# Local attention with a mixture of experts behind it: a tail of at most 32 tokens with the output's columns, in place of the sum, dealt to the four column groups

## The chip, the core and the metric

The kernel runs on one core of one Trainium2 chip. The time is the device time of one execution in microseconds; the number given for a kernel is the median of its runs.

## What is computed

Queries, keys and values have shape 4 x 8 x 768 x 64 (batch, heads, positions, head size). Each position attends to its neighbours closer than 16 positions and to 24 summaries of blocks of 32 positions. The result, read as 3072 tokens of 512 numbers, goes into a layer of eight experts, of which each token takes the two best:

```python
x = attn_out.transpose(0, 2, 1, 3).reshape(3072, 512)
noisy = x @ w_gate + log1p(exp(x @ w_noise)) * noise
top2 = the two largest of noisy per token; top2_w = softmax over those two
for e in range(8):
    for k in range(2):
        mask = top2[:, k] == e
        h = maximum(x[mask] @ w1[e], 0)            # 512 -> 1024
        out[mask] += top2_w[mask, k, None] * (h @ w2[e])   # 1024 -> 512
```

## The kernel before

TensorE (PE) does the attention in 24 tiles of 128 tokens. From about 137 us on the experts are computed, one after the other, the fullest first. Expert e has room for `CAPS[e]` tokens: 800, 832, 808, 800, 784, 776, 768, 768. Its tokens are cut into chunks of 128, and what is over the first 768 is its **tail**, the seventh chunk (`LAST` = 6): 32, 64, 40, 32, 16 and 8 tokens for experts 0 to 5, none for 6 and 7.

For each expert PE makes the hidden values (lines L854 for experts 0 and 1, L1360 for the later ones, which form them by the seven products of Strassen's scheme), ScalarE (ACT) rounds them to f16 in `hth`, and VectorE (DVE) writes the remainder to `htl` (L863, L1395). The second matrix product then goes chunk by chunk into a PSUM bank `pt` (L909, L1432), in three passes of eight matmuls (w2h by hth, w2l by hth, w2h by htl). After a chunk DVE scales it by the gate's weight and adds what other experts have left in the output (`y`, L931; L929 where nothing is added), and GpSimd (POOL) scatters the rows of `y` to the output by an indirect DMA (L90). The rows that are added were gathered by POOL beforehand (`prev`).

A tail does not fill the 128 columns of PE's array, so it is put on parts of the array. With 33 to 64 tokens (experts 1 and 2, lines L906 and L1429) there are two column groups of 64, and each computes half of the output's columns: 48 matmuls of 256 columns. With at most 32 tokens (experts 0, 3, 4 and 5, lines L902 and L1426; the function `four` says which) there are four column groups of 32, and each computes all 512 columns of a quarter of the sum over the hidden values: 24 matmuls of 512 columns. The four partial sums then stand in four groups of 32 partitions, and four operations of DVE add them one after the other:

```python
for g in range(4):
    x = py[32 * g:32 * g + n]
    if g or pv is not None:
        nc.vector.scalar_tensor_tensor(y, x, gw, y if g else pv[:n], op0=OP.mult, op1=OP.add)
```

These are lines L920 and L922. Which rows of the output a 64-wide tail is gathered from and scattered to stands in the table `IL`, and its gate weights in `TL`; `last_ids` (L777, L778) fills both from the table `TB` while PE makes the second half of expert 0's hidden values.

The order of the work is written out by hand, and each engine takes its instructions in that order. Of the loop over f = 0 to 7 for expert 0's second half, each step issues 12 matmuls of PE into one of four banks `h` taken in turn, then ACT's L860, then DVE's L863, which frees the bank. After the step f = 1 DVE also gets the decoding of the token tables (L638 to L694) and `last_ids`; after the steps 2 to 5 a conversion of expert 1's weights (L758). For the experts from 2 on, the first products of the next expert are put ahead of the tail (`seven_head`), and the others follow it; they pass through banks that DVE has to read (L1386, L1388, L1395) before PE can go on writing in them.

Of the kernel before, what the change touches and what calls it, by code (L numbers as in the profile page):

```python
# [8 lines left out]
F32 = mybir.dt.float32  # L9
# [5 lines left out]
OP = mybir.AluOpType  # L15
# [5 lines left out]
P = 128  # L21
TS = S // P
NT = B * TS
N = B * S
DM = H * D
E, F = 8, 1024
# [11 lines left out]
CAPS = (800, 832, 808, 800, 784, 776, 768, 768)  # L38
# [25 lines left out]
def attn_moe(ctx, tc, qt, kt, vt, wgn, noise, w1, w2, out):  # L64
    nc = tc.nc
    PSUM = bass.MemoryType.PSUM

    const = ctx.enter_context(tc.tile_pool(name="const", bufs=1))
# [19 lines left out]
    def indirect(**kw):  # L88
        nc.gpsimd.memset(spacer, 0.0)
        return nc.gpsimd.indirect_dma_start(**kw)  # L90


    LAST = NCH - 1
# [120 lines left out]
    late = []  # L214
# [83 lines left out]
    def bank():  # L298
        return banks[0].tile([P, 1, 512], F32, name="h")
# [206 lines left out]
    TB = const.tile([P, E, NCH, 2], I32, name="tb")  # L506
# [251 lines left out]
        nc.vector.scalar_tensor_tensor(lo, SG[e, i], sc, hi, op0=OP.mult, op1=OP.subtract)  # L758

    XTE = {}  # L760
    HD = DM // 2
    out2 = out.rearrange("n (h d) -> (n h) d", h=2)
    TL = const.tile([P, E, 2], I32, name="tl")
    IL = const.tile([P, E], I32, name="il")
    side = const.tile([P, 1], F32, name="side")

    def last_init():
        nc.gpsimd.memset(TL, OOB)
        nc.gpsimd.memset(side[0:64], 0.0)
        nc.gpsimd.memset(side[64:128], 1.0)  # L770

    def last_ids():
        for c in sorted(set(CAPS)):
            e0, e1 = CAPS.index(c), len(CAPS) - CAPS[::-1].index(c)
            for i in range(2 if c > LAST * P + 32 else 0):
                n = c - LAST * P
                nc.vector.tensor_copy(TL[64 * i:64 * i + n, e0:e1], TB[0:n, e0:e1, LAST, :])  # L777
        nc.vector.tensor_scalar(IL, TL[:, :, 0], 2.0, side, op0=OP.mult, op1=OP.add)  # L778

    def four(e, c):  # L780
        return c == LAST and CAPS[e] - LAST * P <= 32

    def tb_of(e, c):
        return TB0[:, c] if e == 0 and c < 3 else TB[:, e, c]
# [88 lines left out]
    def prev_gather(e, c):  # L873
        n = min(P, CAPS[e] - c * P)
        pv = PREV[pi_[0] % len(PREV)]
        pi_[0] += 1
        if c == LAST and not four(e, c):
            g = indirect(
                out=pv[:, :HD], out_offset=None, in_=out2,
                in_offset=bass.IndirectOffsetOnAxis(ap=IL[:, e:e + 1], axis=0),  # L880
                bounds_check=2 * N - 1, oob_is_err=False)
        else:
            g = indirect(
                out=pv[:n], out_offset=None, in_=out,
                in_offset=bass.IndirectOffsetOnAxis(ap=tb_of(e, c)[:n, 0:1], axis=0),
                bounds_check=N - 1, oob_is_err=False)
        for o in ow.get(e, []):
            tc.declare_no_dep(g.ins, o.ins, reason="an expert's slots hold different tokens")
        ow.setdefault(e, []).append(g)
        return pv  # L890

    def mm2_pass(e, c, py, k, end=2):
        last = c == LAST
        w = WT[e]
        hh, hl = HT
        wn, hx = (("w2h", hh), ("w2h", hl), ("w2l", hh))[k]
        wv = w[wn].rearrange("p a (b d) -> p (a b) d", d=DM)
        for f in range(FC):
            st, sp = k + f == 0, k == end and f == FC - 1
            if four(e, c):  # L900
                g = 32 * (f % 4)
                nc.tensor.matmul(py[g:g + 32], hx[:, f, c * P:c * P + 32], wv[:, f, :], start=k == 0 and f < 4,  # L902
                                 stop=sp, skip_group_check=True)
            elif last:
                for i in range(2):
                    nc.tensor.matmul(py[64 * i:64 * i + 64, :HD], hx[:, f, c * P:c * P + 64],  # L906
                                     wv[:, f, HD * i:HD * i + HD], start=st, stop=sp, skip_group_check=True)
            else:
                nc.tensor.matmul(py, hx[:, f, c * P:c * P + P], wv[:, f, :], start=st, stop=sp)  # L909

    def mm2_out(e, c, py, pv):
        last = c == LAST
        if four(e, c):
            n = CAPS[e] - LAST * P
            y = late[0].tile([P, DM], F32, name="y", bufs=4)[:n]
            gw = tb_of(e, c).bitcast(F32)[:n, 1:2]
            for g in range(4):
                x = py[32 * g:32 * g + n]
                if g or pv is not None:
                    nc.vector.scalar_tensor_tensor(y, x, gw, y if g else pv[:n], op0=OP.mult, op1=OP.add)  # L920
                else:
                    nc.vector.tensor_scalar(y, x, gw, None, op0=OP.mult)  # L922
            y_scatter(e, c, y)
            return
        d = HD if last else DM
        y = late[0].tile([P, DM], F32, name="y", bufs=4)[:, :d]
        gw = (TL[:, e] if last else tb_of(e, c)).bitcast(F32)[:, 1:2]
        if pv is None:
            nc.vector.tensor_scalar(y, py[:, :d], gw, None, op0=OP.mult)  # L929
        else:  # L930
            nc.vector.scalar_tensor_tensor(y, py[:, :d], gw, pv[:, :d], op0=OP.mult, op1=OP.add)  # L931
        y_scatter(e, c, y)
# [5 lines left out]
        mm2_out(e, c, py, pv)  # L938

    def y_scatter(e, c, y):  # L940
        last = c == LAST and not four(e, c)
        n = CAPS[e] - LAST * P if four(e, c) else P
        s = indirect(
            out=out2 if last else out,
            out_offset=bass.IndirectOffsetOnAxis(ap=IL[:, e:e + 1] if last else tb_of(e, c)[:n, 0:1], axis=0),
            in_=y, in_offset=None, bounds_check=(2 * N if last else N) - 1, oob_is_err=False)
        for o in ow.get(e, []):
            tc.declare_no_dep(s.ins, o.ins, reason="an expert's slots hold different tokens")
        ow.setdefault(e, []).append(s)
# [189 lines left out]
    for i in range(3):  # L1139
        x = late[0].tile([P, DM], F32, name=f"prev{i}")  # L1140
# [80 lines left out]
    py = [bank()[:, 0] for c in range(3)]  # L1221
# [34 lines left out]
    def tail(e):  # L1256
        return (CAPS[e] - LAST * P) // 2 if CAPS[e] > LAST * P else 0
# [147 lines left out]
    def cols(e, c, hx, f):  # L1405
        h, k = CAPS[e] // 2, tail(e)
        if c == LAST:
            return hx[:, f, 3 * P:3 * P + (32 if four(e, c) else 64)]
        c0 = P * c if c < 3 else h + k + P * (c - 3)
        return hx[:, f, c0:c0 + P]  # L1410

# [5 lines left out]
    def mm2_part(e, c, py, k, fs, start, stop):  # L1417
        w = G["w2"] if e > 1 else WT[e]
        wn, hx = (("w2h", HT[0]), ("w2h", HT[1]), ("w2l", HT[0]))[k]
        wv = w[wn].rearrange("p a (b d) -> p (a b) d", d=DM)  # L1420
        for f in fs:
            st, sp = start and f == fs[0], stop and f == fs[-1]
            x = cols(e, c, hx, f)
            if four(e, c):
                g = 32 * (f % 4)
                nc.tensor.matmul(py[g:g + 32], x, wv[:, f, :], start=start and f < 4, stop=sp, skip_group_check=True)  # L1426
            elif c == LAST:
                for i in range(2):
                    nc.tensor.matmul(py[64 * i:64 * i + 64, :HD], x, wv[:, f, HD * i:HD * i + HD], start=st,  # L1429
                                     stop=sp, skip_group_check=True)  # L1430
            else:
                nc.tensor.matmul(py, x, wv[:, f, :], start=st, stop=sp, skip_group_check=True)  # L1432

# [55 lines left out]
    for e in range(1, E):  # L1489
        pv = []  # L1490
# [5 lines left out]
        n = e + 1  # L1496
# [45 lines left out]
        else:  # L1542
# [7 lines left out]
            for i in range(1, 5):  # L1550
# [16 lines left out]
                else:  # L1567
                    py = psum.tile([P, 512], F32, name="pt", bufs=2)
# [11 lines left out]
        for c in range(chunks(e)):  # L1580
            if c == chunks(e) - 1 and n < E:
                seven_head(n)
            if c or e == 1:
                py = psum.tile([P, 512], F32, name="pt", bufs=2)
                for i, k in enumerate((0, 2, 1)):
                    if e == 1:
                        mm2_pass(e, c, py, k, 1)
                    else:
                        mm2_part(e, c, py, k, range(FC), i == 0, i == 2)
                    if i < 2:  # L1590
                        hook(32 + 3 * c + i)
            else:
                for k in (2, 1):
                    mm2_part(e, 0, py, k, range(7), False, False)
                    hook(33 - k // 2)
                for k in (0, 2, 1):
                    mm2_part(e, 0, py, k, (7,), False, k == 1)
            mm2_out(e, c, py, pv[c])
            prev()
            hook(34 + 3 * c)  # L1600
# [106 lines left out]
```

## Time and profile before

| | before |
|---|---|
| median of 3 runs | 648.92 us (647.35 to 651.18) |
| profiled execution | 650.73 us, of which the span 648.9 us |
| PE busy | 628.6 us (97% of the span) |
| DVE busy | 481.2 us (74%) |
| ACT busy | 316.1 us (49%) |
| POOL busy | 250.2 us (39%) |

A row of a group of matmuls gives the time from its first start to its last modelled end, and matmuls overlap; so the pace of matmuls is read from the distance of their starts. "Idle before" in square brackets is idle time of that engine just ahead of the row, with what ended it. PEld are loads of stationary weights into PE's array; they run beside matmuls.

### The profile page before, as it was taken

What the parts mean: (1) busy time and instruction counts of PE and PEld (TensorE: products, weight loads), DVE (VectorE), ACT (ScalarE), POOL (GpSimd) and SP (SyncE); (2) the same over time, 40 slices, a digit from 0 to 9 for tenths busy, and PEclk for the clock granted to TensorE, in tenths of its full rate; (3) what the DMA queues carried; (4) which work ended last, traced back from release to release, by engine and by line L of the source; (5) the groups of instructions that cost most, each with busy time, mean ns of one, the idle gap of its engine ahead of it and who ended that gap; (6) DMA issues with size and microseconds to landing.
All of it is one profiled execution on the core that took longest, in us unless ns stands there. A gap on an engine that the chain in (4) does not pass through costs nothing.

```text
span 648.9 us, 14149 instructions
## 1 busy us (share of the span) xinstructions
PE 628.6 (97%) x5295; PEld 363.4 (56%) x5295; DVE 481.2 (74%) x1039; ACT 316.1 (49%) x692; POOL 250.2 (39%) x432
## 2 busy tenths in 40 slices
PE   8989898999999999999999999999999999999995
PEld 7778676765554554465446544554454455445542
DVE  5768598979887599368887887988798679767510
ACT  4878597973054354065436433653465256425300
POOL 4352043202335353623572356326632542333041
PEclk9999798999999999999999999999999999999998
DMA  9999978963639595838786688769776868763021
GB/s 304 325 278 342 307 218 275 299 230 124 198 123 252 166 220 144 282 84 170 185 226 172 168 200 246 181 135 225 236 201 136 221 210 165 175 191 123 3 94 51
DMA packets 123709, 127.93 MB, mean 197 GB/s; under 512 B 83242, under 2 KB 86674, under 8 KB 123630
## 3 DMA queue, kind: packets, MB, share of 16 engines
q1 hardware_dynamic: 111838, 90.66, 52.1%
q0 software_dynamic: 11792, 36.27, 18.2%
q8 instruction: 44, 0.72, 0.5%
q14 instruction: 35, 0.29, 0.2%
HBM read 81.85 MB, written 25.61 MB: 166 GB/s over the span
## 4 chain that ended last, share of the span: by engine, by line
PE 86%; DVE 6%; ACT 3%; DMA 2%; issue 2%; SPq 1%; POOL 0%; POOLq 0%; DVEq 0%; ACTq 0%
PE pt L1432 29%; PE h L1360 16%; PE h L854 10%; PE pt L909 7%; PE pt L1360 3%; PE pt L341 3%; PE o L1360 3%; PE s L318 3%; PE o L354 3%; PE h L909 2%; PE o L246 1%; ACT p L333 1%; PE pt L378 1%; DMA vd<-in_vt_dram 1%; DVE y L920 1%
## 5 line engine op out<-in xcount | busy, mean ns | idle before, releaser
L90 POOL DMA_INDIRECT out_dram<-y,tb x52 | 69.5, 1336 | 165.3 <-DVE y L931 127.7
L90 POOL DMA_INDIRECT xg<-xd,tb x54 | 60.9, 1127 | 118.8 <-DVE rh L1388 31.5
L1432 PEld LDWEIGHTS <-hth 128*128 128x128 f16 x576 | 56.3, 98 | 66.7
L931 DVE SCALAR_TENSOR_TENSOR y<-pt,tb,prev 128x512 f32<-128x512 f32 x42 | 31.5, 749 | 64.9 <-PE pt L1432 54.2
L1360 PEld LDWEIGHTS <-w1h 128*128 128x128 f16 x504 | 48.9, 98 | 38.2 <-issue 4.4
L1432 PE MATMUL pt<-w2l,hth 128*128 128x512 f16 x288 | 69.0, 379 | 0.0
L1432 PE MATMUL pt<-w2h,htl 128*128 128x512 f16 x288 | 69.0, 379 | 0.0
L1432 PE MATMUL pt<-w2h,hth 128*128 128x512 f16 x288 | 69.0, 379 | 0.0
L1360 PEld LDWEIGHTS <-w1l 128*128 128x128 f16 x504 | 49.3, 98 | 34.9
L90 POOL DMA_INDIRECT prev<-out_dram,tb x45 | 52.6, 1169 | 23.9 <-issue 13.2
L333 ACT ACTIVATE p<-s,nm 128x120 f32<-128x120 f32 x192 | 51.1, 377 | 0.8
L854 PE MATMUL h<-xte,w1h 128*128 128x384 f16 (+2 forms) x248 | 49.1, 336 | 0.0
L1432 PEld LDWEIGHTS <-htl 128*128 128x128 f16 x288 | 28.2, 98 | 34.0
L1349 ACT ACTIVATE w1h<-stg 128x768 f16<-128x768 f32 (+1 forms) x24 | 22.7, 944 | 40.6 <-DVE stg L1340 40.6
L1392 ACT ACTIVATE hth<-h 128x384 f16<-128x384 f32 (+4 forms) x48 | 23.8, 497 | 35.5 <-PE h L1360 35.5
L1349 ACT ACTIVATE w1l<-stg 128x768 f16<-128x768 f32 (+1 forms) x24 | 22.5, 942 | 37.3 <-DVE stg L1340 37.3
L1360 PE MATMUL h<-xte,w1h 128*128 128x384 f16 (+4 forms) x180 | 39.7, 329 | 0.7 <-DVE h L1386 0.4
L1360 PE MATMUL h<-xte,w1l 128*128 128x384 f16 (+4 forms) x180 | 39.7, 329 | 0.0
L1313 ACT ACTIVATE x<-xt 128x512 f16<-128x512 f32 (+2 forms) x44 | 26.5, 626 | 23.4 <-issue 19.2
L1340 DVE TENSOR_TENSOR stg<-stg 128x256 f32<-128x256 f32 x96 | 36.3, 419 | 0.8
L344 ACT ACTIVATE pts<-pt 120x512 f32<-120x512 f32 x48 | 26.7, 609 | 19.4 <-PE pt L341 19.4
L854 PEld LDWEIGHTS <-w1h 128*128 128x128 f16 x256 | 24.7, 98 | 19.5 <-issue 1.2
(301 smaller groups left out, 1305.7 us busy)
## 6 DMA issues: line engine op xcount, KB each, us to landing
stg<-in_w_dram SPq DMA_DIRECT2D x64, 512.0 KB
q<-in_qt_dram SPq DMA_DIRECT2D x24, 256.0 KB
xd<-x SPq DMA_DIRECT2D x24, 256.0 KB
out_dram<-xg SPq DMA_DIRECT2D x8, 768.0 KB
kb<-in_kt_dram SPq DMA_DIRECT2D x6, 768.0 KB
hth<-in_vt_dram SPq DMA_DIRECT2D x12, 260.0 KB
htl<-in_vt_dram SPq DMA_DIRECT2D x16, 195.0 KB
ve<-in_vt_dram SPq DMA_DIRECT2D x12, 260.0 KB
```

Source lines behind the costliest of these rows:

```text
L90: return nc.gpsimd.indirect_dma_start(**kw)
L333: nc.scalar.activation(PE_[t][:, a, hp, :], SC[t][:, a, hp, :], AF.Exp, bias=NM[t][:, 1, a, hp:hp + 1], scale=0.125)
L344: nc.scalar.activation(PT[t][:NK, a], pt[:NK], AF.Copy)
L854: nc.tensor.matmul(ph[:, :n], w1_of(w, wn, c, f), x[:, xo + c, c0:c1], start=(k == 0), stop=(k == 11))
L909: nc.tensor.matmul(py, hx[:, f, c * P:c * P + P], wv[:, f, :], start=st, stop=sp)
L931: nc.vector.scalar_tensor_tensor(y, py[:, :d], gw, pv[:, :d], op0=OP.mult, op1=OP.add)
L1313: nc.scalar.activation(t[:r, c:c + k], src, AF.Copy)
L1340: nc.vector.tensor_tensor(o, x, y, op=op)
L1349: nc.scalar.activation(hi, x, AF.Copy, scale=W1S)
L1360: nc.tensor.matmul(ph[:, :h], w[:, la, a, P * j:P * j + P], x[:, j, :h], start=start and k == 0, stop=k == 5, skip_group_check=True)
L1392: nc.scalar.activation(hh[:, f, t], src, AF.Relu)
L1432: nc.tensor.matmul(py, x, wv[:, f, :], start=st, stop=sp, skip_group_check=True)
```

## The change

Tails of at most 32 tokens now work as the 64-wide ones do: each of the four column groups computes a quarter of the output's columns (128) over the whole sum. A tail thus has 96 matmuls of 128 columns, each with a weight load of its own, in place of 24 of 512; DVE evacuates it with one operation on 128 partitions x 128 columns; and rows of 512 bytes, a quarter of an output row, are gathered and scattered by ids in `IL`. `last_ids` fills the tables expert by expert, with four copies for each of the experts 0, 3, 4 and 5, two for 1 and 2, and one operation for the ids of each. The table `side`, set by POOL, has two columns in place of one.

```diff
     def last_ids():
-        for c in sorted(set(CAPS)):
-            e0, e1 = CAPS.index(c), len(CAPS) - CAPS[::-1].index(c)
-            for i in range(2 if c > LAST * P + 32 else 0):
-                n = c - LAST * P
-                nc.vector.tensor_copy(TL[64 * i:64 * i + n, e0:e1], TB[0:n, e0:e1, LAST, :])
-        nc.vector.tensor_scalar(IL, TL[:, :, 0], 2.0, side, op0=OP.mult, op1=OP.add)
+        for e in range(E):
+            n = CAPS[e] - LAST * P
+            if n > 0:
+                q = parts(e)
+                for i in range(0, P, P // q):
+                    nc.vector.tensor_copy(TL[i:i + n, e], TB[0:n, e, LAST, :])
+                nc.vector.tensor_scalar(IL[:, e:e + 1], TL[:, e, 0:1], float(q), side[:, q // 4:q // 4 + 1],
+                                        op0=OP.mult, op1=OP.add)
+
+    def parts(e):
+        return 4 if CAPS[e] - LAST * P <= 32 else 2
...
-            if four(e, c):
-                g = 32 * (f % 4)
-                nc.tensor.matmul(py[g:g + 32], x, wv[:, f, :], start=start and f < 4, stop=sp, skip_group_check=True)
-            elif c == LAST:
-                for i in range(2):
-                    nc.tensor.matmul(py[64 * i:64 * i + 64, :HD], x, wv[:, f, HD * i:HD * i + HD], start=st,
-                                     stop=sp, skip_group_check=True)
+            if c == LAST:
+                q = parts(e)
+                n, d = P // q, DM // q
+                for i in range(q):
+                    nc.tensor.matmul(py[n * i:n * i + n, :d], x, wv[:, f, d * i:d * i + d], start=st, stop=sp,
+                                     skip_group_check=True)
...
-        if four(e, c):
-            n = CAPS[e] - LAST * P
-            y = late[0].tile([P, DM], F32, name="y", bufs=4)[:n]
-            gw = tb_of(e, c).bitcast(F32)[:n, 1:2]
-            for g in range(4):
-                x = py[32 * g:32 * g + n]
-                if g or pv is not None:
-                    nc.vector.scalar_tensor_tensor(y, x, gw, y if g else pv[:n], op0=OP.mult, op1=OP.add)
-                else:
-                    nc.vector.tensor_scalar(y, x, gw, None, op0=OP.mult)
-            y_scatter(e, c, y)
-            return
-        d = HD if last else DM
+        d = DM // parts(e) if last else DM
```

How the order of DVE's instructions moves at the two places of which the prediction speaks:

DVE in expert 0's second half, from the last step of the token tables (L694) to the first remainder behind `last_ids` (`htl`, L863 before and L865 now). Before:

```order
L694 CAST tb<-ids 128x49
L777 COPY tl<-tb 40x2 x2
L777 COPY tl<-tb 64x2 x2
L778 TENSOR_SCALAR il<-tl,side 128x8
L863 SCALAR_TENSOR_TENSOR htl<-h,hth 128x416
```

The same place now:

```order
L694 CAST tb<-ids 128x49
L778 COPY tl<-tb 32x2 x4
L779 TENSOR_SCALAR il<-tl,side 128x1
L778 COPY tl<-tb 64x2 x2
...
L778 COPY tl<-tb 8x2 x4
L779 TENSOR_SCALAR il<-tl,side 128x1
L865 SCALAR_TENSOR_TENSOR htl<-h,hth 128x416
```

Each of the six experts with a tail has a group of copies (L778) with one L779 behind it. The remainder of step f = 2 has 26 operations ahead of it that fill the tables, in place of 5.

DVE around the tail of expert 3 (`y` is the evacuation, `o`, `h` and `pt` are PSUM banks of expert 4's products, L1353 and L1340 convert weights). Before:

```order
L1353 SCALAR_TENSOR_TENSOR w1l_2961<-stg,w1l_2961 128x1024
L920 SCALAR_TENSOR_TENSOR y<-pt,tb,prev_2970 32x512
L920 SCALAR_TENSOR_TENSOR y<-pt,tb,y 32x512 x3
L1395 SCALAR_TENSOR_TENSOR htl<-o,hth 128x392
L1386 TENSOR_TENSOR h<-h,p_5853 128x392
L758 SCALAR_TENSOR_TENSOR w2l_322<-stg,w2h_321 128x1024 x2
L1388 TENSOR_TENSOR rh_3827<-h,p_5853 128x392
```

Now:

```order
L1340 SCALAR_TENSOR_TENSOR w1l_2967<-stg,w1l_2967 128x1024
L919 SCALAR_TENSOR_TENSOR y<-pt,tl,prev_2976 128x128
L1382 SCALAR_TENSOR_TENSOR htl<-o,hth 128x392
L1373 TENSOR_TENSOR h<-h,p_5949 128x392
L758 SCALAR_TENSOR_TENSOR w2l_322<-stg,w2h_321 128x1024 x2
L1375 TENSOR_TENSOR rh_3923<-h,p_5949 128x392
```

Three operations are gone from between the tail and expert 4's first remainder; the rest stands as it did.

## Rows read from the trace of the kernel before

**Rows 1.** The page's busy time of each engine, with its share of the span and its count of instructions.

```profile
PE 628.6 (97%) x5295; PEld 363.4 (56%) x5295; DVE 481.2 (74%) x1039; ACT 316.1 (49%) x692; POOL 250.2 (39%) x432
```

**Rows 2.** Busy time by stage: the stretch, its length, busy time and count of PE, PEld, DVE, ACT and POOL, PE's clock as a share of full speed, the DMA engines' share, GB/s. The first stretch holds expert 0's second half and its second product, the others reach from tail to tail.

```profile
175.00:210.00 35.00, 35.00 (x210) 17.98 (x208) 28.67 (x57) 15.78 (x23) 15.05 (x23) 1.00 0.71 180
343.00:404.00 61.00, 61.00 (x337) 31.00 (x338) 50.15 (x87) 30.45 (x52) 29.63 (x46) 1.00 0.75 190
404.00:465.00 61.00, 60.70 (x337) 30.91 (x336) 52.18 (x90) 30.28 (x52) 29.79 (x46) 1.00 0.77 194
465.00:526.00 61.00, 60.64 (x341) 31.07 (x339) 48.66 (x84) 28.12 (x48) 25.25 (x42) 1.00 0.76 197
526.00:588.00 62.00, 61.57 (x331) 32.22 (x330) 49.42 (x86) 29.83 (x51) 20.05 (x30) 1.00 0.69 172
```

**Rows 3.** The chain that ended last: start, length on the chain, engine and line. The tails of experts 0, 2 and 3.

```profile
208.50 1.41 PE pt L902 x24
...
340.24 2.74 PE pt L1429 x48
...
402.55 1.44 PE pt L1426 x24
```

**Rows 4.** The timeline of all engines from the tail of expert 3: start, length (us), engine, line, operation, output<-inputs, shape, count, and idle time ahead of it.

```profile
403.89 0.84 PE L1360 MATMUL o<-xte,w1h 128*128 128x392 f16 x4
404.01 0.74 DVE L920 SCALAR_TENSOR_TENSOR y<-pt,tb,prev 32x512 f32<-32x512 f32 x1 [1.53 <-PE pt L1426]
...
404.78 2.31 DVE L920 SCALAR_TENSOR_TENSOR y<-pt,tb,y 32x512 f32<-32x512 f32 x3
...
407.13 0.57 DVE L1395 SCALAR_TENSOR_TENSOR htl<-o,hth 128x392 f16<-128x392 f32 x1
...
407.55 0.49 PE L1360 MATMUL h<-xl,w1l 128*128 128x392 f16 x2
407.61 0.56 DVE L1386 TENSOR_TENSOR h<-h,p 128x392 f32<-128x392 f32 x1
...
408.08 2.35 DVE L758 SCALAR_TENSOR_TENSOR w2l<-stg,w2h 128x1024 f16<-128x1024 f32 x2
408.23 0.82 PE L1360 MATMUL h<-xte,w1h 128*128 128x392 f16 x4 [0.19 <-DVE h L1386]
...
413.86 0.49 PE L1360 MATMUL o<-xl,w1h 128*128 128x392 f16 x2
414.47 0.82 PE L1360 MATMUL h<-xte,w1h 128*128 128x392 f16 x4
```

**Rows 5.** PE's timeline at the same two places behind the tail of expert 5.

```profile
529.36 0.49 PE L1360 MATMUL h<-xl,w1l 128*128 128x384 f16 x2
...
530.10 0.81 PE L1360 MATMUL h<-xte,w1h 128*128 128x384 f16 x4 [0.25 <-DVE h L1386]
...
535.62 0.49 PE L1360 MATMUL o<-xl,w1h 128*128 128x384 f16 x2
536.29 0.81 PE L1360 MATMUL h<-xte,w1h 128*128 128x384 f16 x4 [0.18 <-DVE htl L1395]
```

**Rows 6.** Line L931 of DVE: count, shortest, median and longest duration in ns, starts, shapes.

```profile
L931 DVE SCALAR_TENSOR_TENSOR y<-pt,tb,prev x42: 732/751/753, 251.2 to 641.6; 128x512 f32<-128x512 f32 x42
L931 DVE SCALAR_TENSOR_TENSOR y<-pt,tl,prev x2: 484/484/485, 280.2 to 343.0; 128x256 f32<-128x256 f32 x2
```

**Rows 7.** DVE's timeline around `last_ids` and at the remainder of step f = 7, and L777's line of durations.

```profile
185.66 0.69 DVE L777 COPY tl<-tb 40x2 int32<-40x2 int32 x4
186.46 0.23 DVE L778 TENSOR_SCALAR il<-tl,side 128x8 int32<-128x8 int32 x1
186.60 0.58 DVE L863 SCALAR_TENSOR_TENSOR htl<-h,hth 128x416 f16<-128x416 f32 x1
...
196.43 0.58 DVE L863 SCALAR_TENSOR_TENSOR htl<-h,hth 128x416 f16<-128x416 f32 x1
...
L777 DVE COPY tl<-tb x4: 160/162/164, 185.7 to 186.2; 40x2 int32<-40x2 int32 x2, 64x2 int32<-64x2 int32 x2
```

**Rows 8.** PE's timeline in the same stretch: the last four matmuls of step f = 5 with the first four of f = 6, and the third pass of chunk 3, which reads the remainders.

```profile
187.88 1.57 PE L854 MATMUL h<-xte,w1h 128*128 128x416 f16 x8
...
196.25 1.89 PE L909 MATMUL pt<-w2h,htl 128*128 128x512 f16 x8
```

**Rows 9.** Starts of matmuls on column groups: the tail of expert 3 (first pass, and its weight loads as PEld), and the attention's 64-column matmuls, which go in turn to two column groups.

```profile
402.48 0.61 PE L1426 MATMUL pt<-w2h,hth 128*32 128x512 f16 x8
402.48 0.34 PEld L1426 LDWEIGHTS <-hth 128*32 128x32 f16 x12 [0.32 <-issue]
...
402.92 0.60 PE L1426 MATMUL pt<-w2l,hth 128*32 128x512 f16 x8
...
59.06 0.22 PE L354 MATMUL o<-ve,pts 120*64 120x65 f32 x1
59.07 0.22 PE L354 MATMUL o<-htl,pts 120*64 120x65 f32 x1
59.12 0.22 PE L354 MATMUL o<-ve,pts 120*64 120x65 f32 x1
...
59.88 0.22 PE L354 MATMUL o<-ve,pts 120*64 120x65 f32 x1
```

**Rows 10.** The stretch of the attention in which loads and matmuls stood densest, columns as in rows 2.

```profile
37.32:40.15 2.83, 2.83 (x102) 2.55 (x102) 0.54 (x3) 2.30 (x9) 0.00 (x0) 1.00 1.04 338
```

More of the change, by code (lines that the diff above doesn't have):

```diff
@@ L760, in attn_moe @@
     XTE = {}
-    HD = DM // 2
-    out2 = out.rearrange("n (h d) -> (n h) d", h=2)
+    outs = {q: out.rearrange("n (h d) -> (n h) d", h=q) for q in (2, 4)}
     TL = const.tile([P, E, 2], I32, name="tl")
     IL = const.tile([P, E], I32, name="il")
-    side = const.tile([P, 1], F32, name="side")
+    side = const.tile([P, 2], F32, name="side")
     def last_init():
         nc.gpsimd.memset(TL, OOB)
-        nc.gpsimd.memset(side[0:64], 0.0)
-        nc.gpsimd.memset(side[64:128], 1.0)
+        for i in range(4):
+            for k in range(2):
+                nc.gpsimd.memset(side[32 * i:32 * i + 32, k:k + 1], float(i if k else i // 2))
     def last_ids():
-        for c in sorted(set(CAPS)):
-            e0, e1 = CAPS.index(c), len(CAPS) - CAPS[::-1].index(c)
-            for i in range(2 if c > LAST * P + 32 else 0):
-                n = c - LAST * P
-                nc.vector.tensor_copy(TL[64 * i:64 * i + n, e0:e1], TB[0:n, e0:e1, LAST, :])
-        nc.vector.tensor_scalar(IL, TL[:, :, 0], 2.0, side, op0=OP.mult, op1=OP.add)
-    def four(e, c):
-        return c == LAST and CAPS[e] - LAST * P <= 32
+        for e in range(E):
[8 more added lines that the diff above has]
+        return 4 if CAPS[e] - LAST * P <= 32 else 2
     def tb_of(e, c):
@@ L876, in prev_gather @@
         pi_[0] += 1
-        if c == LAST and not four(e, c):
+        if c == LAST:
             g = indirect(
-                out=pv[:, :HD], out_offset=None, in_=out2,
+                out=pv[:, :DM // parts(e)], out_offset=None, in_=outs[parts(e)],
                 in_offset=bass.IndirectOffsetOnAxis(ap=IL[:, e:e + 1], axis=0),
-                bounds_check=2 * N - 1, oob_is_err=False)
+                bounds_check=parts(e) * N - 1, oob_is_err=False)
         else:
@@ L899, in mm2_pass @@
             st, sp = k + f == 0, k == end and f == FC - 1
-            if four(e, c):
-                g = 32 * (f % 4)
-                nc.tensor.matmul(py[g:g + 32], hx[:, f, c * P:c * P + 32], wv[:, f, :], start=k == 0 and f < 4,
-                                 stop=sp, skip_group_check=True)
-            elif last:
-                for i in range(2):
-                    nc.tensor.matmul(py[64 * i:64 * i + 64, :HD], hx[:, f, c * P:c * P + 64],
-                                     wv[:, f, HD * i:HD * i + HD], start=st, stop=sp, skip_group_check=True)
+            if last:
+                q = parts(e)
+                n, d = P // q, DM // q
+                for i in range(q):
+                    nc.tensor.matmul(py[n * i:n * i + n, :d], hx[:, f, c * P:c * P + n],
+                                     wv[:, f, d * i:d * i + d], start=st, stop=sp, skip_group_check=True)
             else:
@@ L940, in y_scatter @@
     def y_scatter(e, c, y):
-        last = c == LAST and not four(e, c)
-        n = CAPS[e] - LAST * P if four(e, c) else P
+        last = c == LAST
         s = indirect(
-            out=out2 if last else out,
-            out_offset=bass.IndirectOffsetOnAxis(ap=IL[:, e:e + 1] if last else tb_of(e, c)[:n, 0:1], axis=0),
-            in_=y, in_offset=None, bounds_check=(2 * N if last else N) - 1, oob_is_err=False)
+            out=outs[parts(e)] if last else out,
+            out_offset=bass.IndirectOffsetOnAxis(ap=IL[:, e:e + 1] if last else tb_of(e, c)[:, 0:1], axis=0),
+            in_=y, in_offset=None, bounds_check=(parts(e) * N if last else N) - 1, oob_is_err=False)
         for o in ow.get(e, []):
@@ L1407, in cols @@
         if c == LAST:
-            return hx[:, f, 3 * P:3 * P + (32 if four(e, c) else 64)]
+            return hx[:, f, 3 * P:3 * P + P // parts(e)]
         c0 = P * c if c < 3 else h + k + P * (c - 3)
@@ L1423, in mm2_part @@
             x = cols(e, c, hx, f)
-            if four(e, c):
-                g = 32 * (f % 4)
-                nc.tensor.matmul(py[g:g + 32], x, wv[:, f, :], start=start and f < 4, stop=sp, skip_group_check=True)
-            elif c == LAST:
-                for i in range(2):
-                    nc.tensor.matmul(py[64 * i:64 * i + 64, :HD], x, wv[:, f, HD * i:HD * i + HD], start=st,
-                                     stop=sp, skip_group_check=True)
+            if c == LAST:
+                q = parts(e)
+                n, d = P // q, DM // q
+                for i in range(q):
+                    nc.tensor.matmul(py[n * i:n * i + n, :d], x, wv[:, f, d * i:d * i + d], start=st, stop=sp,
+                                     skip_group_check=True)
             else:
```

## The prediction

> **What bounds the kernel now.** I read the page's busy times first: PE is busy for 97% of the span and DVE for 74% [rows 1]. An average does not say which of them a change of a tail touches, so the busy time by stage came next: in expert 0's second half and from expert 2's tail to expert 3's PE has no idle time at all, and in the three stretches behind the tails of experts 3, 4 and 5 it has 0.30, 0.36 and 0.43 us [rows 2]. The clock there is 1.00, the level of 2.4 GHz. So in these stages PE's work is the time: a microsecond more on PE is a microsecond at the end, and a microsecond saved on DVE is worth something only where PE waits for it. The chain of waits shows what a tail costs PE: 1.41 to 1.44 us with four column groups, 2.74 with two [rows 3]. The timelines then show where PE waits for DVE.
>
> **The change, part by part.**
>
> *PE in the tails.* Now four matmuls, one on each column group, start together: eight make a pass, and the passes start at 402.48 and 402.92, so two fours take 0.43 us and one 0.216, which is 512 columns at 2.4 GHz (213 ns) and 2 to 3 ns. Twelve weight loads start within the first 0.34 us less one load's length, ahead of the matmuls that need them [rows 9]. Of the 1.44 us six fours take 1.30; 0.14 is the drain at the end. After the change there are 24 fours of 128 columns. If columns set the pace, a four takes 53 ns and 2.5, and the tail 24 x 0.056 + 0.14 = 1.48 us: 0.04 more than now. If loads and matmuls come at the densest pace that the attention holds over as many of them, 102 pairs in 2.83 us or 27.7 ns a pair [rows 10], the tail takes 96 x 0.0277 + 0.14 = 2.80 us, 1.4 more. Those are the two ends. Between them the nearest row is the attention's 64-column product: two column groups start 7 to 10 ns apart, each with its own load, and the next two follow after 58 to 59 ns (14 steps from 59.06 to 59.88) [rows 9]. Two loads of 64 columns in that time are as many columns of weights as four of 32. I take 58.6 ns for a four: 24 x 0.0586 + 0.14 = 1.55 us, **0.1 us more a tail and 0.4 for four.**
>
> The Trainium skill speaks against the change here: "TensorE: Matmul & The Clock Gate", Part 3, has it that LDWEIGHTS overlaps with matmuls in flight only where the row groups differ, and here all four column groups use all rows; by its formula for LDWEIGHTS a load of 32 columns takes 27 ns, so 96 of them would take 2.6 us, an estimate from that page, and the four tails would cost 5 us more in place of 0.4. The trace speaks against the rule: twelve loads start beside eight matmuls of the same rows [rows 9].
>
> *DVE behind the tails.* The first of four evacuations starts at 404.01 and the last ends at 407.09, 3.08 us in all [rows 4]. One operation of 128 partitions x 128 columns takes their place. The operation takes 751 ns for 512 columns and 484 for 256 [rows 6]; the same slope gives 484 - 134 = 350 ns for 128. So DVE is free 2.7 us earlier. What that is worth is read from PE: behind expert 3's tail the remainder L1395 waits until 407.13 for the chain, L1386 follows at 407.61, and PE, whose next matmul would start at 407.55 + 2 x 0.165 = 407.88, starts at 408.23, after L1386: 0.35 us lost. The two conversions L758 behind it pass the delay on, and at 414.47 PE loses another 0.28 (414.19 was due) [rows 4]. Behind expert 5's tail the same two losses are 0.42 (529.68 due, 530.10 done) and 0.35 (535.94 due, 536.29 done) [rows 5]. For expert 4 I take the mean, 0.70. Together 2.1 us. Behind the two-way tail of expert 2, where one operation of 484 ns evacuates [rows 6], PE has no idle time [rows 2]; so all of it should go: **-2.1 us.** If PE's tail becomes longer, DVE only has more time, and nothing else is late next: L1386 then waits for PE's own product. Expert 0's tail has no such loss to give back [rows 2].
>
> *The tables.* `last_ids` has 26 small operations on DVE where it had 5. The four copies, the wait and the operation for the ids took from 185.66 to 186.60, 0.94 us [rows 7]. After the change four experts need such a group each, and two need one with two copies less (a copy is 0.16 to 0.18 us): 4 x 0.94 + 2 x 0.60 = 4.96, which is 4.0 us more. Copies at their bare 162 ns and ids in 0.14 would give 3.1 more; a third of a microsecond for every operation of ids with its wait, 4.7. Queued behind them is DVE's whole line, without a gap from there to the remainder of step f = 7 [rows 7]. Who waits for it: step f = 6 of PE writes in the bank that the remainder of f = 2 frees. That remainder ends at 186.60 + 0.58 = 187.18, and f = 6 starts at 187.88 + 4 x 0.175 = 188.58 [rows 7, 8]: 1.4 us of cover. The next edge is tighter: the remainder of f = 7 ends at 197.01 [rows 7], and the third pass of chunk 3 wants it in its last matmul, at 196.25 + 7 x 0.216 = 197.76 [rows 8]; with the load ahead of it some 0.6 us of cover. PE thus stands still for 4.0 - 1.4 = 2.6 us at f = 6 and for 0.8 more in chunk 3: **+3.4 us** (2.5 to 4.1 by the two ends), and from there to 404 us no idle time of PE takes it up [rows 2].
>
> *The rest.* Six more small memsets on POOL stand at the end of the attention, where nothing waits for POOL's tables until `last_ids`, 55 us later. Gathers and scatters of a tail now have 128 rows of 512 bytes; they are hidden by the distance between a tail and its next reader, half an expert. I cost both at nothing.
>
> **The sum:** +0.4 - 2.1 + 3.4 = **+1.7 us**, on the profiled execution 650.73 + 1.7 = 652.4. That execution lies 1.8 above the median of the runs shown, so the forecast against the median is 648.92 + 1.7 = **650.6 us**, 0.3% slower, which a measurement of this kernel, that can tell about 0.5% (3.2 us) from no change, would call the same.
>
> **The rivals.**
>
> *Pace of small pairs (0.25).* PE cannot feed a load and a matmul to its column groups every 14 ns, and the tails run at the pace of rows 10: 1.4 us more each, 5.6 for four. Then 5.6 - 2.1 + 3.4 = +6.9, 655.8 us. It decides for slower by 0.5% from a tail of 1.44 + (3.2 + 2.1 - 3.4)/4 = 1.92 us on, a pair each 18.5 ns. For it: no stretch of the attention shows a denser run as long. Against it: those stretches are full with their own columns, so they bound the pace from above only. The skill's rule above is of this kind.
>
> *Stalls stay (0.13).* The losses behind the tails come from the conversions L758 as much as from the evacuation, and PE keeps them: 0.4 + 3.4 = +3.8, 652.7 us. Against it: the stretch behind the two-way tail, with the same conversions, has no idle time [rows 2].
>
> *Tables hidden (0.10).* The small operations overlap so far, or the bank is free so early, that PE does not wait: 0.4 - 2.1 = -1.7, 647.2 us, faster but less than can be told. Against it: DVE's line has no gap in which to make 3 us good.
>
> **How the numbers follow.** The forecast has 0.52 and by its own bounds (2.5 to 4.1 for the tables, 0.04 to 0.3 a tail) reaches from 649.2 to 652.2. The range is to take in the third case, half of the second's way from the forecast to 655.8, and the spread of a median: **647.8 to 655.0**. What is left out is the lower half of "tables hidden" and the full price of the pace. Slower by over 0.5% is nearly all of the pace, most of "stalls stay" and a tail of the forecast: 0.36. Faster by over 0.5% would need tables at no cost and more gain than the losses add up to: 0.04. The same: 0.60.
>
> **What would show it right or wrong.** The four tails on the chain: 1.5 us each by the forecast, 2.8 by the pace. PE's idle time behind the tails of experts 3, 4 and 5: none. In step f = 6 of expert 0's second half: PE idle for 2 to 3 us on DVE's remainder, and again for under 1 us in the third pass of chunk 3. The one evacuation: about 350 ns. The forecast is wrong if a tail is over 1.9 us, if the idle time behind the tails stays, or if PE runs through f = 6.

## The result, and the profile after

| | median us | ratio to before (95%) |
|---|---|---|
| before | 647.14 | |
| changed | 650.79 | 1.0055 (1.0035 to 1.0076) |

The changed kernel is 3.65 us slower, 0.55%, and the interval of the ratio does not take in 1. The forecast was 650.6 and the median lies within its range, but as a difference the forecast was +1.7 us. That the median comes out 0.2 us from the forecast is luck: the median of before, over more executions, is 1.8 us lower than the one the forecast started from. So the difference is what has to be explained. The profiled executions differ by about the same amount: 654.55 us (span 652.8) against 650.73 (span 648.9).

The page of the changed kernel, busy time of each engine, for [rows 1]:

```profile
PE 627.0 (96%) x5583; PEld 364.7 (56%) x5583; DVE 475.7 (73%) x1048; ACT 316.6 (48%) x692; POOL 251.8 (39%) x438
```

PE has 288 matmuls more, 96 for 24 in each of four tails, and is not busy for longer; DVE is busy 5.5 us less. The span is 3.9 us longer all the same, so the time went into waiting.

The busy time by stage, with the columns of [rows 2]:

```profile
175.00:214.00 39.00, 36.08 (x285) 18.93 (x284) 33.13 (x78) 15.86 (x23) 14.70 (x23) 1.00 0.71 158
404.00:465.00 61.00, 60.17 (x405) 31.46 (x403) 48.84 (x87) 29.47 (x52) 29.50 (x47) 1.00 0.80 194
465.00:526.00 61.00, 60.52 (x410) 31.91 (x409) 46.78 (x81) 29.05 (x49) 25.76 (x44) 1.00 0.79 193
526.00:588.00 62.00, 61.91 (x421) 32.95 (x420) 46.21 (x80) 28.96 (x50) 22.20 (x32) 1.00 0.75 183
```

Expert 0's second half now has 2.92 us without a matmul, where it had none. The other three stretches still have idle time, but it has moved, as the timelines below show.

DVE's timeline around `last_ids`, for [rows 7]:

```profile
185.19 0.67 DVE L778 COPY tl<-tb 32x2 int32<-32x2 int32 x4
...
190.12 0.21 DVE L779 TENSOR_SCALAR il<-tl,side 128x1 int32<-128x1 int32 x1
190.25 0.58 DVE L865 SCALAR_TENSOR_TENSOR htl<-h,hth 128x416 f16<-128x416 f32 x1
```

And PE's at step f = 6 and in the third pass of chunk 3, for [rows 8]:

```profile
187.60 0.87 PE L856 MATMUL h<-xte,w1h 128*128 128x416 f16 x4
190.89 0.34 PE L856 MATMUL h<-xte,w1h 128*128 128x416 f16 x1 [2.42 <-DVE htl L865]
...
200.73 0.39 PE L909 MATMUL pt<-w2h,htl 128*128 128x512 f16 x1 [0.50 <-DVE x L815]
```

DVE's remainder of step f = 7, which that last matmul reads:

```profile
200.09 0.58 DVE L865 SCALAR_TENSOR_TENSOR htl<-h,hth 128x416 f16<-128x416 f32 x1
```

`last_ids` now holds DVE from 185.19 to 190.25, 5.06 us. The remainder behind it ends at 190.83, and the next matmul starts at 190.89 after 2.42 us of waiting. In the third pass of chunk 3 the last matmul waits 0.50 us. The row names L815, DVE's operation just ahead of the remainder of f = 7; the remainder itself ends at 200.67, 0.06 us before the matmul starts.

The chain that ended last at the tail of expert 0 and, piece by piece, the tail of expert 3, for [rows 3]:

```profile
211.48 1.45 PE pt L906 x96
...
405.50 0.78 PE pt L1415 x46
...
406.29 0.53 PE pt L1415 x23
406.82 0.35 issue
407.18 0.28 PE pt L1415 x4
407.45 0.46 issue
407.92 0.53 PE pt L1415 x23
```

Expert 0's 96 matmuls take 1.45 us, 0.04 more than its 24 took. Expert 3's take 2.95. "issue" is time in which PE waits for nothing that the profile shows: no semaphore holds it, and the next matmul of the same tail comes late.

PE, POOL and DVE around that tail, for [rows 4, 9]; POOL's lines are its indirect transfers, and their length is the time of the issue:

```profile
404.78 1.53 POOL L90 DMA_INDIRECT xg<-xd,tb  x1 [0.22 <-issue]
...
405.43 0.63 PE L1415 MATMUL pt<-w2h,hth 128*32 128x128 f16 x32
...
405.89 0.87 PE L1415 MATMUL pt<-w2l,hth 128*32 128x128 f16 x32
...
406.62 1.01 POOL L90 DMA_INDIRECT out_dram<-y,tb  x1 [0.22 <-issue]
407.18 0.28 PE L1415 MATMUL pt<-w2h,htl 128*32 128x128 f16 x4 [0.35 <-issue]
...
408.49 0.35 DVE L919 SCALAR_TENSOR_TENSOR y<-pt,tl,prev 128x128 f32<-128x128 f32 x1 [3.05 <-PE pt L1415]
```

The one evacuation takes 0.35 us, as forecast. The gather at 404.78 ends at 406.31, and PE's first halt ends at 406.29; the scatter at 406.62 ends at 407.63, and the last halt ends 0.29 later. The halt between them ends at 407.18, while the scatter is still being issued, and only four pairs run before the next. That coincidence was read out of the trace only after the first experiments; it is what the later ones test.

**The account.** PE's matmuls outside the four-way tails are the same in both kernels, so the start of one and the same matmul can be compared between the two traces:

| the matmul | before | after | lag | change of the lag |
|---|---|---|---|---|
| step f = 1 of expert 0's second half | 177.66 | 177.39 | -0.27 | |
| first of chunk 3 | 192.80 | 195.10 | +2.30 | +2.57, tables |
| tail of expert 0 | 208.43 | 211.41 | +2.98 | +0.68, tables |
| first behind it | 209.84 | 212.87 | +3.03 | +0.05 |
| tail of expert 3 | 402.48 | 405.43 | +2.95 | -0.08 |
| first behind it | 403.89 | 408.38 | +4.49 | +1.54, tail |
| tail of expert 4 | 463.53 | 467.40 | +3.87 | -0.62, losses gone |
| first behind it | 464.94 | 469.66 | +4.72 | +0.85, tail |
| tail of expert 5 | 524.37 | 528.40 | +4.03 | -0.69, losses gone |
| first behind it | 525.78 | 530.19 | +4.41 | +0.38, tail |
| last of the kernel | | | +3.66 | -0.75, losses gone |

Tables +3.25, tails +2.82, losses behind the tails -2.06, the rest -0.08: +3.93 from the first row on. The forecast had +3.4, +0.4 and -2.1. One of its three terms failed.

### The profile page after: what moved, and what is told of

It reads as the page before. It is cut to its first block, busy times and chain, and to the rows that moved or that the text cites. A ratio compares the mean times of both kernels' runs of the same rounds, so it can differ in the third digit from the quotient of the medians.

```text
span 652.8 us, 14739 instructions
## 1 busy us (share of the span) xinstructions
PE 627.0 (96%) x5583; PEld 364.7 (56%) x5583; DVE 475.7 (73%) x1048; ACT 316.6 (48%) x692; POOL 251.8 (39%) x438
## 4 chain that ended last, share of the span: by engine, by line
PE 86%; DVE 7%; DMA 4%; issue 2%; ACT 1%; SPq 0%; POOL 0%; POOLq 0%; DVEq 0%; ACTq 0%
PE pt L1418 29%; PE h L1347 18%; PE h L856 9%; PE pt L909 7%; PE o L1347 4%; PE pt L1347 4%; PE h L909 2%; PE pt L341 2%; PE o L354 2%; PE s L318 2%; DMA htl<-in_vt_dram 2%; PE pt L1415 1%; PE pt L378 1%; DMA stg<-in_w_dram 1%; DVE nm L325 1%
## 5 line engine op out<-in xcount | busy, mean ns | idle before, releaser
L90 POOL DMA_INDIRECT out_dram<-y,tb x48 | 66.6, 1387 | 152.0 <-DVE y L919 131.2
L90 POOL DMA_INDIRECT prev<-out_dram,tb x42 | 48.6, 1156 | 28.0 <-issue 12.8
L1382 DVE SCALAR_TENSOR_TENSOR htl<-h,hth 128x384 f16<-128x384 f32 (+4 forms) x48 | 26.7, 564 | 12.4 <-ACT hth L1379 11.1
```

Source lines behind the costliest of these rows:

```text
L1382: nc.vector.scalar_tensor_tensor(hl[:, f, t], src, 0.0, hh[:, f, t], op0=OP.max, op1=OP.subtract)
```

## The experiments

The median of each kernel, the ratio to before on the same chip, and how much its lag against before grows in the two traces from step f = 1 of expert 0's second half to the last matmul:

| kernel | median us | ratio (95%) | growth of the lag, us |
|---|---|---|---|
| changed | 650.79 | 1.0055 (1.0035 to 1.0076) | +3.93 |
| e1_shift | 650.52 | 1.0047 (1.0021 to 1.0073) | +4.19 |
| e2_spread | 652.60 | 1.0073 (1.0047 to 1.0098) | +8.13 |
| e3_tables_late | 647.46 | 1.0003 (0.9981 to 1.0025) | +1.51 |
| e4_one_evacuation | 644.27 | 0.9960 (0.9932 to 0.9988) | -2.09 |
| e5_pool_after | 647.30 | 1.0010 (0.9985 to 1.0034) | +2.02 |
| e6_pool_copies | 650.05 | 1.0060 (1.0026 to 1.0094) | +2.08 |
| e7_both | 643.67 | 0.9948 (0.9919 to 0.9977) | -2.11 |
| e8_tail0_late | 650.96 | 1.0094 (1.0059 to 1.0129) | +4.01 |

Before was 647.14 beside the changed kernel and e1 to e4, and 646.28 beside e5 to e8. The attention varies by some us between executions: at step f = 1 of expert 0's second half the profiled execution of e1_shift was 6.85 us ahead of that of before, with the same work but the warm-up. So terms of a few tenths are read from the lag between matmuls, not from the medians.

**e1_shift: is it a place in PE's stream?**

```
-    warm_up(WARM)
+    warm_up(WARM - 24)
+    for i in range(86):
+        nc.tensor.matmul(VO[0][:, i % 2, 0:8], identb, identb[:, 0:8], ...
```

> The changed kernel with 62 more pairs of load and matmul on PE: 24 of the 100 warm-up pairs become 86 pairs of 8 columns, so everything behind them stands 124 instructions later in PE's stream, and the work is the same. Theory A (PE takes its instructions in blocks of 256, the 16 kB packets of queue q8, and halts where a block ends; in a tail of 192 short instructions the halt shows): the halts move by 62 pairs. They stood after 73, 32 and 45 pairs of the tails of experts 3, 4 and 5 and 2 matmuls behind that of expert 0; they would stand after 11 pairs of expert 3's tail (hidden by the instructions queued ahead), before those of experts 4 and 5 or at their ends, and after some 35 pairs of expert 0's. Tails of 1.5 us for experts 3 to 5 in place of 2.95, 2.25 and 1.79, and 2.0 to 2.3 for expert 0 in place of 1.45. The whole: 1.5 to 2.5 us less than the changed kernel, if the attention's halts don't move against it. Theory B (the instructions ahead are used up and new ones come at a fixed pace): nothing moves; 2.9, 2.3, 1.8 us again and 1.45 for expert 0.

Measured, PE and POOL around the tail of expert 3:

```profile
397.98 1.53 POOL L90 DMA_INDIRECT xg<-xd,tb  x1 [0.22 <-issue]
...
398.62 0.63 PE L1417 MATMUL pt<-w2h,hth 128*32 128x128 f16 x32
...
399.81 1.01 POOL L90 DMA_INDIRECT out_dram<-y,tb  x1 [0.22 <-issue]
400.39 0.28 PE L1417 MATMUL pt<-w2h,htl 128*32 128x128 f16 x4 [0.38 <-issue]
...
401.16 0.55 PE L1417 MATMUL pt<-w2h,htl 128*32 128x128 f16 x25 [0.50 <-issue]
```

The halts stand after 46, 67 and 71 pairs; they had stood after 46, 69 and 73, and should have moved by 62. In the tail of expert 4 they stand after 24 and 29 pairs in place of 32, in that of expert 5 after 35 in place of 45. Theory A has fallen. Expert 0's tail has none again, 1.45 us.

**e2_spread: long matmuls between the passes.**

```
-            if c == chunks(e) - 1 and n < E:
+            apart = e > 1 and c == LAST and parts(e) == 4
+            if c == chunks(e) - 1 and n < E and not apart:
                 seven_head(n)
...
                     if i < 2:
                         hook(32 + 3 * c + i)
+                        if apart:
+                            seven(n, 0, (1, 5)[i])
```

> The changed kernel, but the two products of the next expert (6 matmuls of 384 to 392 columns each, about 1 us each) that stand ahead of the tails of experts 3, 4 and 5 stand between the tail's three passes. Both theories of the halts inside the tails have it that PE's queue is full again after 1 us of long matmuls; a pass is 32 pairs, 0.45 us. Each pass is then 0.45 to 0.5 us, the 2.8 us of halts in the three tails go to under 0.6, and the time is 2 to 2.8 us under the changed kernel (about 648.3 where that is 650.8). If the halts come from something else (DVE or ACT at the same memory, the bank that the tail writes), they stay: no difference.

Measured: both theories had expected it faster, and it is not. The median is 1.8 us above that of the changed kernel, which the two intervals don't tell apart. In the traces the three tails cost 6.2 us of lag, where those of the changed kernel cost 2.8. POOL at expert 3's tail:

```profile
401.22 1.22 POOL L90 DMA_INDIRECT xg<-xd,tb  x1 [0.22 <-issue]
...
402.82 1.73 POOL L90 DMA_INDIRECT out_dram<-y,tb  x1 [0.29 <-issue]
```

And PE there:

```profile
401.35 0.68 PE L1415 MATMUL pt<-w2h,hth 128*32 128x128 f16 x32
403.24 0.33 PE L1347 MATMUL o<-xte,w1h 128*128 128x392 f16 x1 [1.22 <-issue]
403.96 0.66 PE L1347 MATMUL o<-xte,w1h 128*128 128x392 f16 x3 [0.40 <-issue]
...
404.88 0.63 PE L1415 MATMUL pt<-w2l,hth 128*32 128x128 f16 x32
```

After one pass of 32 pairs PE halts in front of long matmuls, for 1.22 and 0.40 us, and goes on at its full pace afterwards. These long matmuls write another bank (`o`, not `pt`), and the profile shows no semaphore that they wait for, so what is late seems to be not a matmul's data or bank but the instruction itself, whatever its size. A reading that fits: the first pass, now 2 us earlier, has used up what PE held while POOL issues a gather and a scatter. Theory B, a fixed pace, does not fit either: behind the halts 32 pairs run in 0.45 us. Laying the halts of all kernels beside POOL's timeline gave theory D, as e5_pool_after puts it.

**e3_tables_late: the tables alone.**

```
-    def last_ids():
-        for e in range(E):
+    def last_ids(es):
+        for e in es:
...
-            last_ids()
+            last_ids((0,))
...
             on(0, tail_ids)
+            on(1, last_ids, (1, 2))
+            on(2, last_ids, (3, 4))
+            on(3, last_ids, (5,))
```

> The changed kernel, but only expert 0's group of last_ids (4 copies and one operation, 0.8 us) stays where it was; the other 21 small operations stand in the first half of expert 1, where DVE has idle time. My theory: step f = 6 and the third pass of chunk 3 have no idle time any more, so 3.2 us less than the changed kernel, 647.5 where that is 650.8. Rival (DVE's line is late anyway, and PE finds the next thing late): under 1.5 us less.

Measured: 3.3 us less than the changed kernel (647.46 and 650.79, both beside 647.14), and both waits are gone. Expert 0's second half, columns as in [rows 2]:

```profile
175.00:207.00 32.00, 32.00 (x261) 16.90 (x259) 25.81 (x52) 15.34 (x22) 14.44 (x21) 1.00 0.75 184
```

PE has no idle time there, and none in the 34 us behind it, into which the 21 operations have gone: where DVE has time they cost nothing. In the lag the whole is only 2.4 us less. The tables' 3.25 are gone, but the tails cost 1.0 more: expert 4's now meets a gather and a scatter of POOL as expert 3's does, halts after 46, 70 and 74 pairs and takes 3.00 us.

**e4_one_evacuation: the losses behind the tails alone.**

```
-            for g in range(4):
+            for g in range(1):
                 x = py[32 * g:32 * g + n]
```

> The kernel before with the first of the four evacuations of each four-way tail alone; the other three quarters of those tails' sums are left out. The matmuls and the tables are those of before. My theory: PE's losses behind the tails of experts 3, 4 and 5 (0.63, 0.69 and 0.75 us) go, 2.1 us less than before, 645.1 where that is 647.1. Rival (the conversions behind the tail cause them as much): under 1 us less, and the idle times stay in part.

Measured: 0.9960, 2.6 us less than before (0.8 to 4.4); in the lag between matmuls it is 2.1, at the very places of [rows 4, 5]. The stretches behind the tails of experts 3 and 5:

```profile
399.00:460.00 61.00, 61.00 (x349) 31.13 (x342) 49.90 (x87) 30.80 (x54) 28.54 (x47) 1.00 0.80 198
...
520.00:582.00 62.00, 62.00 (x338) 32.67 (x335) 48.02 (x83) 30.76 (x53) 20.09 (x30) 1.00 0.71 174
```

No idle time is left, nor in the one between. The conversions L758 are still there, so "stalls stay" falls.

**e5_pool_after: POOL's transfers away from the tails.**

```
-        y_scatter(e, c, y)
+        if e > 1 and c == LAST - 1 and CAPS[e] > LAST * P and parts(e) == 4:
+            held.append((e, c, y))
+        else:
+            y_scatter(e, c, y)
+            while held:
+                y_scatter(*held.pop())
...
-            on(42 if e == 1 else 47, xs_gather, n + 1, 1)
+            on(42 if e == 1 else 52 if CAPS[e] > LAST * P and parts(e) == 4 else 47, xs_gather, n + 1, 1)
```

> The changed kernel, with POOL's indirect transfers kept away from the tails of experts 3, 4 and 5: the scatter of chunk 5 stands behind the tail's scatter in POOL's line, and the two gathers of the expert after next behind both. PE's and DVE's lines are as they were. Theory D (while POOL issues an indirect transfer, PE gets hardly any new instructions and lives on those it holds, some 64, which a tail uses up in 0.45 us; in the traces so far the halts inside the tails end within 0.3 us of the end of such an issue): no halts, the three tails take 1.5 us each in place of 2.95, 2.25 and 1.79; 2.5 us less than the changed kernel, 648.3 where that is 650.8. Theory B (the instructions that PE holds run out after its own waits, whatever POOL does): 2.9, 2.3 and 1.8 us again, no difference.

Measured, the chain at the three tails:

```profile
403.66 1.45 PE pt L1422 x96
...
464.14 1.45 PE pt L1422 x96
...
524.34 1.45 PE pt L1422 x96
```

PE and POOL at the first of them:

```profile
403.59 0.63 PE L1422 MATMUL pt<-w2h,hth 128*32 128x128 f16 x32
...
404.49 0.62 PE L1422 MATMUL pt<-w2h,htl 128*32 128x128 f16 x32
...
405.80 1.00 POOL L90 DMA_INDIRECT out_dram<-y,il  x1 [5.05 <-DVE y L919]
```

The halts of all three tails are gone with nothing changed on PE: 1.45 us each in place of 2.95, 2.25 and 1.79. The ratio went from 1.0055 to 1.0010, 2.9 us. In the lag it is 1.9: the tails' 2.6, less 0.8 that the tables cost more in this execution, as the last section shows. One part of theory D is too strong: not every earlier halt ended within 0.3 us of the end of an issue. The one that ended at 407.18 in the changed kernel, and both at expert 3's tail of e2_spread, ended in the middle of one, so an issue lets a few instructions through.

**e6_pool_copies: POOL busy, without a transfer.** As e5_pool_after, with

```
             held.append((e, c, y))
+            for i in range(2):
+                nc.gpsimd.tensor_copy(y, y)
```

> As the kernel with the transfers moved away, but where the scatter of chunk 5 stood POOL copies that chunk's y onto itself twice, so POOL is busy in the same stretch, and with no transfer. Theory D, if it is the issue of the transfer that counts: tails of 1.5 us each, as without the copies. If it is enough that POOL works: halts of 0.3 to 0.7 us in each of the three tails as in the changed kernel.

Measured, POOL and PE at the tail of expert 3:

```profile
399.82 2.21 POOL L923 COPY y<-y 128x512 f32<-128x512 f32 x2 [1.88 <-DVE y L919]
...
400.88 0.63 PE L1424 MATMUL pt<-w2h,hth 128*32 128x128 f16 x32
...
401.78 0.62 PE L1424 MATMUL pt<-w2h,htl 128*32 128x128 f16 x32
```

The copies run until 402.03, beside the first two passes and the start of the third, and there is no halt: it is the transfer, not that POOL works. That it is the issue and not the data on the way is seen in the trace of the changed kernel: no packet of POOL's queue is under way during the first halt of expert 3's tail (406.06 to 406.29), whose gather is still being issued. No packet of instructions is under way during any halt of its tails either. And traffic of other queues alone does no harm: beside the tail of expert 3 in e5_pool_after (403.60 to 404.90) the DMA engines moved 315 GB/s. The lag of e6_pool_copies grows by as much as that of e5_pool_after. Why its median is 2.75 us above that kernel's is not explained by this trace and stays open.

**e8_tail0_late: the halt brought to the tail that had none.**

```
-        mm2(0, c, None)
+        if c < LAST:
+            mm2(0, c, None)
...
+            on(0, mm2, 0, LAST, None)
             on(0, tail_ids)
```

> The changed kernel with expert 0's tail, the one without halts, one step of expert 1's first product (12 matmuls, 2 us) later, so that it meets POOL's scatter of chunk 5, which ran from 1.1 to 2.8 us after the end of that chunk. Theory D: a halt of 0.4 to 0.8 us inside the tail, which takes 1.9 to 2.3 us in place of 1.45, and PE goes on when the scatter's issue has ended. Theory B: the step ahead of it has no wait that the chunk ahead of it had not, so no halt and 1.45 us.

Measured, POOL and PE at the tail of expert 0:

```profile
207.02 1.71 POOL L90 DMA_INDIRECT out_dram<-y,tb  x1 [3.37 <-DVE y L917]
...
207.83 0.63 PE L906 MATMUL pt<-w2h,hth 128*32 128x128 f16 x32
208.29 0.91 PE L906 MATMUL pt<-w2l,hth 128*32 128x128 f16 x32
...
208.99 0.66 PE L906 MATMUL pt<-w2h,htl 128*32 128x128 f16 x32
```

The second pass takes 0.91 us in place of 0.62, and the third starts 0.70 behind it in place of 0.44: a halt of 0.27, which ends with the scatter's issue at 208.73. From its first matmul to the first behind it (209.58) the tail takes 1.75 us in place of 1.46 (211.41 to 212.87). The sign is theory D's, the size is under its 0.4 to 0.8: half of the issue, until 207.83, passed beside the long matmuls of the step ahead.

**e7_both: the two remedies together.** The edits of e3_tables_late and e5_pool_after.

> The changed kernel with both mended: the groups of last_ids for experts 1 to 5 in the first half of expert 1, and POOL's transfers behind the tails of experts 3 to 5. By theory D and the tables' 3.3 us: 650.8 - 3.3 - 2.5 = 645.0, some 2 us under the kernel before (0.3%). By theory B: 647.5, as with the tables alone.

Measured, the stretches behind the tails of experts 3 and 5:

```profile
395.00:456.00 61.00, 61.00 (x412) 31.99 (x411) 50.33 (x90) 30.41 (x53) 28.81 (x46) 1.00 0.80 197
...
516.00:578.00 62.00, 62.00 (x422) 33.03 (x421) 46.19 (x80) 28.90 (x50) 22.43 (x34) 1.00 0.72 184
```

PE has no idle time in them, nor in the one between. 643.67 us, 0.9948 of before (0.9919 to 0.9977): this version beats both kernels, before by 3.4 us (1.5 to 5.2). In the traces its lag shrinks by 2.11 us: the losses behind the tails are gone, and nothing has come in their place.

## Why the prediction was right and where it failed

**PE in the tails: the step that failed.** The size of an undisturbed tail was right: 1.45 us on the chain, where 1.55 was taken and 1.48 was the lower end by columns. In the tail of expert 4 of e5_pool_after the fours start 56.3 ns apart (23 steps in 1.294 us), 14.1 ns a pair, which is the pace by columns that the lower end had. What failed is "0.1 us more a tail and 0.4 for four": the four measured 0.05, 1.54, 0.85 and 0.38, 2.82 in all. The working priced what PE does with an instruction and took it for granted that the instruction is there. A tail of 48 instructions seems to have lived on what PE held: before, a scatter was issued right into expert 3's tail, whose matmuls kept their pace [rows 9]. POOL's timeline of the kernel before:

```profile
401.84 1.52 POOL L90 DMA_INDIRECT out_dram<-y,tb  x1 [0.22 <-issue]
```

192 instructions in 1.3 us halt beside one. "Pace of small pairs" forecast the same sign, but by another mechanism, a tail of 2.8 us from PE itself; e5_pool_after, with the same matmuls at 1.45, rules that out. The Trainium skill, "TensorE: Matmul & The Clock Gate", Part 3, has it that loads overlap only with matmuls of other row groups. The trace differs, and decides: 96 loads of all 128 rows and their matmuls take 1.45 us here.

**DVE behind the tails: right.** -2.1 forecast, -2.06 in the account, -2.1 in the lag of e4_one_evacuation. The evacuation: 350 ns forecast, 0.35 measured. PE's timeline at the first of the two places behind expert 3's tail, for [rows 4]:

```profile
412.04 0.49 PE L1347 MATMUL h<-xl,w1l 128*128 128x392 f16 x2
412.37 0.83 PE L1347 MATMUL h<-xte,w1h 128*128 128x392 f16 x4
```

The last row starts 2 x 0.165 us behind the one above it, where it had come 0.35 later.

**The tables: right.** DVE is held 5.06 us in place of 0.94, 4.1 more where 4.0 was forecast. At f = 6 PE lost 2.57 (2.6 forecast), in chunk 3 0.68 (0.8 forecast); together 3.25 for 3.4, and in e3_tables_late both waits are gone. "Tables hidden" falls.

**The rest.** The memsets and the form of the transfers cost nothing that the account shows. "Gathers and scatters of a tail ... are hidden" was true of their data: no wait for them shows. It overlooked that the issue of those already there reaches PE. One sum of the working is off: its bounds for the tables and the tails reach from 649.5 to 652.1, not from 649.2 to 652.2. The forecast does not hang on it.

**The sum.** +3.4 + 0.4 - 2.1 was +1.7; it is +3.25 + 2.82 - 2.06 - 0.08 = +3.9 in the profiled executions and +3.65 between the medians. The chance was put at 0.60 for the same and 0.36 for slower; the outcome lies on the line between them.

## What to carry to other kernels

Splitting work into more and shorter instructions can make an engine halt that is fast enough for them: look what stands on POOL's line beside a dense burst, and put its indirect transfers ahead of or behind it. Small operations on an engine that another waits for cost their length less the cover that the waiting engine has (here 4.1 us less 0.9); the same ones were free two stages later. To tell terms of a few tenths apart in a kernel that varies by several us, compare the start of the same matmul in two traces.

## What the runs showed of the hardware

- While POOL issues an indirect transfer (1.0 to 1.7 us), a dense burst on PE halts: it ran 24 to 46 pairs of a tail and then stood still, for 0.2 to 1.2 us at a time. That PE then gets hardly any new instructions and lives on those it holds is the reading that fits; no row shows what it holds. What in the issue holds it up is not shown; only that copies on POOL don't.
- A load and a matmul on each of four column groups sustain 14.1 ns a pair over 96 pairs (e5_pool_after), twice the densest pace of the attention [rows 10].
- After the same wait of 2.4 us at f = 6 PE's clock was granted at 1.00 in the profiled executions of the changed kernel, e1_shift and e8_tail0_late, but at about half, the level of 1.2 GHz, in those of e2_spread, e5_pool_after and e6_pool_copies. Why it differs is not shown. The stretch at the wait, columns as in [rows 2], of the changed kernel:

```profile
188.00:191.00 3.00, 0.58 (x4) 0.25 (x3) 2.82 (x13) 2.02 (x3) 2.56 (x5) 1.00 0.66 180
```

  And of e5_pool_after:

```profile
188.00:191.50 3.50, 3.17 (x10) 1.40 (x10) 3.50 (x6) 0.00 (x0) 0.95 (x2) 0.51 0.71 195
```

  There the tables cost 4.1 us in the lag, not 3.25: the matmuls at the lower clock add 1.5, and the wait in chunk 3 goes.
- The attention has halts of another kind, some of them in both kernels at the same instructions of PE. Counted in the trace's records, the two longest that both have stand ahead of PE's instructions 1474 and 3522, 2048 apart. In the chain of the changed kernel they are the steps named issue at 40.88 (1.24 us) and 95.56 (1.69 us). In e1_shift, with 124 instructions more ahead, a halt of 1.5 us stands at the same count of 1474, ahead of other work (L257 in place of L341); at 3522 it has none.
  The Trainium skill, "Runtime: NRT & Kernel Launch", Instruction fetch mechanics, says that an engine's instructions come in blocks of 256 and that a block's edge is mostly hidden. 2048 is eight times 256, which agrees; but halts of 1.24 and 1.69 us are not hidden. This was the source of theory A, which is wrong for the tails.
